# The first batch's softmax over tokens in the other batches' layout, with x loaded ahead of most weights

## The chip, the cores and the metric

The kernel runs on one core of a Trainium2 chip. The metric is the device time of one execution in microseconds, lower is better. The engines are TensorE (PE, with its weight loads PEld), VectorE (DVE), ScalarE (ACT), GpSimd (POOL) and SyncE (SP, which issues the DMAs here).

## The reference

Four sequences of 12608 tokens with 128 channels go through two stages: attention to 32 inducing points, and a channel mix.

```python
B, N, m, C = 4, 12608, 32, 128
scale = 1.0 / np.sqrt(C)
def mab(q, kv):
    s = scale * (q @ kv.transpose(0, 2, 1))
    s = s - s.max(-1, keepdims=True)
    a = np.exp(s)
    a /= a.sum(-1, keepdims=True) + 1e-09
    return a @ kv
h = mab(I, x)            # I: the inducing points; softmax over all tokens
x = mab(x, h)            # softmax over the 32 points, token by token
x_prev = np.concatenate([zeros((B, 1, D)), x[:, :-1, :]], axis=1)
xk = mu_k * x + (1.0 - mu_k) * x_prev
xr = mu_r * x + (1.0 - mu_r) * x_prev
k = np.maximum(xk @ w_k, 0.0)          # w_k: 128 x 1024
v = k * k @ w_v                        # w_v: 1024 x 128
out = 1.0 / (1.0 + np.exp(-(xr @ w_r))) * v
```

x is float32. The weights of the channel mix come as float64; each is turned into float32 on the chip.

## The kernel before

A batch is cut into six blocks of 2048 tokens (four groups of 512) and a tail of 320. Stage A (softmax over tokens) reads a block: x is transposed to channels by tokens (`xt`), the 32 inducing points give scores for four token parts that lie on four sets of 32 partitions, a running maximum is kept, the exponentials are turned back and multiplied with x. Their sum and the product (`acc`) are rescaled when the maximum grows. `combine` makes `hT` and the mixed products `h4k`, `h4r`, from which the folded weights `W` (parts for k, and 128 columns for the gate) are made by `wpart`. Stage B (softmax over the 32 points) gives per group a tile `R`. The channel mix is a loop of 400 units, four for each group: `up` (four matmuls from `R` and `W`), `square` (DVE evacuates with a Relu to `k_t`, ACT squares twice, POOL subtracts to `kl`), and four units later `down`. ScalarE, DVE and POOL all work for each unit, and everything else is hung between units by number (`at`, `soon`).

The order is written out by hand: every engine runs its instructions in the order in which the code issues them. For batches 1 to 3 stages A and B run between the units of the batch before (`stage_a`, `stage_b`). For batch 0 there is nothing to hide behind: `head()` runs its stage A alone, `start()` its first softmax over the points and its weights, and then the units begin. In `head()` the conversion of the float64 weights is also done: `work` is a list of small steps (six for each of five weight parts: exponent L103, mantissa L113, clamp L107, sign L118, low L121, power L125 with POOL's product L131; and two `split_wv` steps), and `place(n)` issues the next n of them. `PARTS` says how many at which point.

In batch 0 the tokens of a group lie 128 apart per step in x's tiles (`(k p) c`, rows of 512 bytes). In batches 1 to 3 a partition holds 16 tokens in a row (`(p s) c`), and the four parts of a block's scores are then not the four groups. Because batch 0's parts had running maxima of their own, `maxes()` takes the maximum over the four parts at the end and `weights()` rescales.

Of the kernel before, what the change touches and what calls it, by code (L numbers as in the profile page):

```python
# [19 lines left out]
def kernel(  # L20
# [62 lines left out]
    def load_weight(dst, src, n, raw):  # L83
# [11 lines left out]
        def steps():  # L95
# [10 lines left out]
            def clamp():  # L106
                v.tensor_scalar(out=X.t, in0=X.t, scalar1=1151.0, scalar2=-896.0, op0=ALU.min, op1=ALU.add)  # L107
                nc.scalar.activation(out=X.t, in_=X.t, func=AF.Relu)
# [101 lines left out]

    def stage_a_head(j):


# [1 line left out]
        first = j == NBLK - 1
        gr = groups(j)
        w = gr[0][1]
        nk = (w + P - 1) // P
        pw = min(w, P)
        L = Batch()  # L220

        def tr():
            for h in range(0, Q, 2):
                ps = pa.tile([P, 2, G], F32, name="ps_a")
                for i in range(2):
                    for k in range(nk):
                        nc.tensor.transpose(out=ps[:, i, k * pw:(k + 1) * pw], in_=S.xn[j, h + i][:pw, k, :],  # L227
                                            identity=ident[:pw, :pw])
                for i in range(2):
                    dst = xt_tile(S, j, h + i)  # L230
                    if h + i > 0 or not first:
                        nc.scalar.copy(out=dst[:, :w], in_=ps[:, i, :w])
# [9 lines left out]
        def maxi():  # L242
            L.mx = sm.tile([P, 1], F32, name="mx1", bufs=4)
            nc.vector.tensor_reduce(out=L.mx, in_=L.s1[:, :w], op=ALU.max, axis=AX.X)
# [3 lines left out]
            nc.vector.tensor_scalar(out=L.nb, in0=L.mx, scalar1=-scale, scalar2=None, op0=ALU.mult)
# [15 lines left out]
        def etrans():  # L264
            L.ep = pb_tile()
            for k in range(nk):
                nc.tensor.transpose(out=L.ep[:pw, k * P:(k + 1) * P],
                                    in_=L.e1t[:, k * pw:(k + 1) * pw], identity=ident)

        def ecopy():  # L270
            L.e1 = st.tile([P, Q, P], F32, name="e1")
            nc.vector.tensor_copy(out=L.e1[:pw, :nk, :],
                                  in_=L.ep[:pw, :nk * P].rearrange("p (k a) -> p k a", a=P))

        def sums():
            if not first:
                nc.vector.scalar_tensor_tensor(out=S.sum, in0=S.sum, scalar=L.al, in1=L.ss,
                                               op0=ALU.mult, op1=ALU.add)

        def hmm():  # L280
            ps = L.hp = pb_tile()
            for k in range(nk):
                for i in range(Q):
                    nc.tensor.matmul(out=ps[M * i:M * (i + 1), :C],
                                     lhsT=L.e1[:pw, k, M * i:M * (i + 1)],
                                     rhs=S.xn[j, i][:pw, k, :],
                                     start=(k == 0), stop=(k == nk - 1))
            for i in range(Q):
                S.xn.pop((j, i), None)

        def acc():
            if first:
                nc.vector.tensor_copy(out=S.acc, in_=L.hp[:, :C])
            else:
                nc.vector.scalar_tensor_tensor(out=S.acc, in0=S.acc, scalar=L.al,
                                               in1=L.hp[:, :C], op0=ALU.mult, op1=ALU.add)
# [2 lines left out]
        L.ecopy, L.sums, L.hmm, L.acc = ecopy, sums, hmm, acc
# [173 lines left out]
    def combine(b, at=None, t=0):  # L473
# [3 lines left out]
        def maxes():  # L477
            bank = next(banks)
            ps = pb_tile(bank)
            nc.tensor.transpose(out=ps[:1, :P], in_=S.mrun, identity=ident)  # L480
            mg = sm.tile([1, M], F32, name="mg")
            nc.vector.tensor_reduce(out=mg, in_=ps[:1, :P].rearrange("p (i m) -> p m i", i=Q), op=ALU.max, axis=AX.X)
            ps2 = pb_tile(bank)
            for i in range(Q):
                nc.tensor.matmul(out=ps2[M * i:M * (i + 1), :1], lhsT=mg, rhs=one, start=True, stop=True)
            nm = sm.tile([P, 1], F32, name="nm")
            nc.vector.tensor_scalar(out=nm, in0=ps2[:, :1], scalar1=-scale, scalar2=None, op0=ALU.mult)
            L["nm"] = nm

        ahead = at is None  # L490

        def weights():
            ws = S.sum
            if ahead:
                wt = sm.tile([P, 1], F32, name="wt")
                nc.scalar.activation(out=wt, in_=S.mrun, func=AF.Exp, bias=L["nm"], scale=scale)
                ws = sm.tile([P, 1], F32, name="ws")
                nc.vector.tensor_tensor(out=ws, in0=S.sum, in1=wt, op=ALU.mult)
            ps = pb_tile(None if ahead else "b")
            nc.tensor.matmul(out=ps[:, :1], lhsT=stack_f, rhs=ws, start=True, stop=True)  # L500
# [570 lines left out]
```

## Time and profile before

| | us |
|---|---|
| median of 3 runs | 1143.24 (1142.75 to 1146.4) |
| span of the profiled execution | 1141.9 |
| PE busy | 1100.8 |
| POOL busy | 948.5 |
| maximum of batch 0's first full block (L244) | 19.78 |
| hT (L521) | 50.13 |
| first evacuation of the loop (L792) | 60.22 |

The profiled execution is one more run: its own time is known as the span, from its first to its last instruction; the three runs of the first row are timed from outside and lie 0.9 to 4.5 us above that span. Rows of a profile name a line of the kernel, the engine, the operation, and the tiles as out<-in; durations are in us, means of one in ns.

### The profile page before, as it was taken

How to read it: one execution, taken by the hardware profiler on the slowest of the kernel's cores; microseconds unless marked ns; L12 is line 12 of the kernel's file. 1: busy time of each engine (PE TensorE's matmuls, PEld its weight loads, DVE VectorE, ACT ScalarE, POOL GpSimd, SP SyncE). 2: the span in 40 equal slices, each digit the busy share in tenths (PEclk: the TensorE clock that was granted, in tenths of full speed). 3: DMA queues.
4: the chain of work that ended last, by engine and by line, in shares of the span. 5: the costliest groups of instructions: out<-in, count | busy, mean ns of one | idle time of the engine just before them, and what ended most of it. 6: DMA issues, size and time to landing. Idle time of an engine off the chain costs nothing.

```text
span 1141.9 us, 17672 instructions
## 1 busy us (share of the span) xinstructions
PE 1100.8 (96%) x5710; PEld 836.7 (73%) x5710; DVE 917.5 (80%) x1294; ACT 971.6 (85%) x1107; POOL 948.5 (83%) x413
## 2 busy tenths in 40 slices
PE   6788999999989999999999999999999999999997
PEld 4466777777777777777777777777778777777886
DVE  4787899887678988887777889898777888887665
ACT  4487888888988888888987988889889988889996
POOL 1157888988877988888889888888888899999996
PEclk9989999999999999999999999999999999999999
DMA  9213454555135455555134455545222233242212
GB/s 268 75 29 92 106 111 108 127 129 106 33 67 119 94 124 123 125 120 124 23 63 86 110 127 121 131 96 125 49 51 60 45 65 59 54 74 56 43 28 34
DMA packets 274988, 102.32 MB, mean 90 GB/s; under 512 B 234288, under 2 KB 249808, under 8 KB 272592
## 3 DMA queue, kind: packets, MB, share of 16 engines
q1 hardware_dynamic: 274560, 101.18, 40.8%
q8 instruction: 45, 0.74, 0.3%
q14 instruction: 47, 0.39, 0.1%
q10 hardware_dynamic: 336, 0.02, 0.0%
HBM read 28.07 MB, written 25.82 MB: 47 GB/s over the span
## 4 chain that ended last, share of the span: by engine, by line
PE 80%; DVE 9%; ACT 7%; issue 3%; DMA 1%; SPq 0%; DVEq 0%; ACTq 0%
PE ps_v L811 40%; PE ps_a L780 15%; PE ps_a L782 13%; DVE k_t L792 3%; PE pb_b L617 2%; PE ps_v L769 2%; PE ps_v L770 2%; PE pb_a L359 2%; PE pb_a L428 2%; ACT kh L797 2%; ACT L772 1%; ACT L634 1%; ACT k_t L798 1%; DVE kh L794 1%; PE ps_a L227 1%
## 5 line engine op out<-in xcount | busy, mean ns | idle before, releaser
L800 POOL TENSOR_TENSOR kl<-k_t,kh 128x1024 fp32r<-128x1024 f32 (+2 forms) x400 | 939.6, 2377 | 151.7 <-ACT k_t L798 131.2
L792 DVE TENSOR_SCALAR k_t<-ps_a 128x1024 f32<-128x1024 f32 (+1 forms) x400 | 480.4, 1201 | 153.9 <-PE ps_a L782 144.2
L798 ACT ACTIVATE k_t<-k_t 128x1024 f32<-128x1024 f32 (+1 forms) x400 | 418.6, 1049 | 38.6 <-DVE kh L794 22.2
L797 ACT ACTIVATE kh<-k_t 128x1024 fp32r<-128x1024 f32 (+1 forms) x352 | 366.1, 1040 | 89.5 <-PE ps_v L811 49.8
L780 PE MATMUL ps_a<-R,W 128*128 128x512 f32 (+1 forms) x800 | 325.2, 407 | 8.8 <-DMA R<-al 4.7
L782 PE MATMUL ps_a<-R,W 128*128 128x512 f32 (+1 forms) x800 | 314.7, 394 | 0.0
L811 PE MATMUL ps_v<-kh,wvh 128*128 128x512 f32 (+1 forms) x800 | 250.2, 394 | 5.3 <-ACT rT L772 4.7
L811 PE MATMUL ps_v<-kl,wvh 128*128 128x512 f32 (+1 forms) x800 | 249.1, 392 | 0.2 <-POOL kl L800 0.2
L811 PE MATMUL ps_v<-kh,wvl 128*128 128x512 f32 (+1 forms) x800 | 249.2, 392 | 0.0
L780 PEld LDWEIGHTS ps_a<-R,W 128*128 128x128 f32 x800 | 151.7, 190 | 82.9 <-issue 20.0
L811 PEld LDWEIGHTS ps_v<-kh,wvh 128*128 128x128 f32 x800 | 149.7, 189 | 44.0 <-ACT rT L772 9.9
L811 PEld LDWEIGHTS ps_v<-kl,wvh 128*128 128x128 f32 x800 | 150.3, 189 | 34.8 <-POOL kl L800 0.4
L811 PEld LDWEIGHTS ps_v<-kh,wvl 128*128 128x128 f32 x800 | 150.6, 189 | 34.2
L782 PEld LDWEIGHTS ps_a<-R,W 128*128 128x128 f32 x800 | 151.7, 190 | 30.8
L816 DVE TENSOR_TENSOR oT<-ps_v,rT 128x512 f32<-128x512 f32 (+1 forms) x100 | 66.7, 667 | 2.3
L827 DVE STREAM_TRANSPOSE ot<-oT 128x512 f32<-128x512 f32 x96 | 67.3, 701 | 0.0
L794 DVE SCALAR_TENSOR_TENSOR kh<-ps_a,k_t 128x1024 fp32r<-128x1024 f32 x48 | 58.8, 1225 | 5.4 <-DVE k_t L792 0.5
L772 ACT ACTIVATE rT<-ps_v 128x512 f32<-128x512 f32 (+1 forms) x99 | 57.3, 579 | 0.3
L331 DVE STREAM_TRANSPOSE xs<-xb 128x512 f32<-128x512 f32 x72 | 50.0, 695 | 3.6 <-DMA xt<-xs 1.8
L769 PE MATMUL ps_v<-R,W 128*128 128x512 f32 (+1 forms) x99 | 39.1, 395 | 1.4 <-DVE oT L816 1.4
L772 ACT ACT_TABLE_LOAD x31 | 39.8, 1283 | 0.5
L770 PE MATMUL ps_v<-R,W 128*128 128x512 f32 (+1 forms) x99 | 38.7, 391 | 0.0
(192 smaller groups left out, 609.5 us busy)
## 6 DMA issues: line engine op xcount, KB each, us to landing
out_dram<-ot SPq DMA_DIRECT2D x184, 128.0 KB, 3.3
xb<-in_x_dram SPq DMA_DIRECT2D x18, 1024.0 KB, 5.5
xt<-xs SPq DMA_DIRECT2D x288, 64.0 KB, 2.0
R<-ah SPq DMA_DIRECT2D x184, 64.0 KB, 2.0
R<-al SPq DMA_DIRECT2D x184, 64.0 KB, 2.0
kh<-in_x_dram SPq DMA_DIRECT2D x4, 512.0 KB, 7.9
kl<-in_x_dram SPq DMA_DIRECT2D x4, 512.0 KB, 7.5
xb<-in_x_dram SPq DMA_DIRECT2D x8, 256.0 KB, 5.3
```

The lines of the kernel that those rows point to most:

```text
L769: nc.tensor.matmul(out=ps[:, :w], lhsT=S.W[0][:, F:WF], rhs=R[:, 1:w + 1], start=True, stop=False)
L772: nc.scalar.activation(out=self.rT, in_=ps[:, :w], func=AF.Sigmoid)
L780: nc.tensor.matmul(out=ps[:, c, :w], lhsT=S.W[0][:, cs], rhs=R[:, 1:w + 1], start=True, stop=False)
L782: nc.tensor.matmul(out=ps[:, c, :w], lhsT=S.W[1][:, cs], rhs=R[:, 0:w], start=False, stop=True)
L792: nc.vector.tensor_scalar(out=k, in0=self.ps[:, :, :w], scalar1=0.0, scalar2=None, op0=ALU.max)
L794: nc.vector.scalar_tensor_tensor(out=kh, in0=self.ps[:, :, :w], scalar=0.0, in1=k, op0=ALU.max, op1=ALU.mult)
L797: nc.scalar.activation(out=kh, in_=k, func=AF.Square)
L798: nc.scalar.activation(out=k, in_=k, func=AF.Square)
L800: return lambda eng, a, z: eng.tensor_tensor(out=kl[:, :, a:z], in0=k[:, :, a:z], in1=kh.bitcast(F32)[:, :, a:z], op=ALU.subtract)
L811: nc.tensor.matmul(out=self.v, lhsT=wt[:, fc, :], rhs=kk[:, c, :], start=(fc == 0 and n == 0), stop=(fc == FC - 1 and n == 2))
L816: nc.vector.tensor_tensor(out=self.oT, in0=self.v, in1=self.rT, op=ALU.mult)
L827: nc.vector.transpose(out=ot[:, o:o + w], in_=self.oT)
```

## The change

Batch 0 gets the layout of the other batches: a block's loads read `(p s) c`, in two halves of eight tokens a partition (block 0 in four quarters), and the loads of x go first, with one weight part behind each of blocks 1 to 3 and the rest last. A block's transposes are copied out by ACT in two instructions of 1024 elements and not four of 512, into one tile for the block. The maximum is joined over the four parts in each block (five one-element steps on DVE), as in the other batches, and `maxes()` and its rescaling go. The turn of the exponentials is done by DVE alone (L282) and not by PE and a copy. The tail has its own small path. The clamp of the weight conversion goes to POOL. In `start()` the first group's softmax runs alone, the second's behind it, with the maxima, sums and quotients in PSUM. The gate's products (`gates`), the conversion of w_r and of the second half of w_v, and both splits move into units 0 and 1 of the loop.

PE at the start of `head()`. kh, kl and xb hold x, xl its tail; ps_a takes transposes, ps_v scores. Before:

```order
L227 MATMUL ps_a<-ident,xl 128x80 x4
L227 MATMUL ps_a<-ident,kh 128x128 x16
L239 MATMUL ps_v<-xtl,indT 32x80 x4
L227 MATMUL ps_a<-ident,kh 128x128 x16
L267 MATMUL pb_b<-ident,rT 80x128
L239 MATMUL ps_v<-xt,indT 32x512 x4
```

And now:

```order
L223 MATMUL ps_a<-ident,xl 128x80 x4
L229 MATMUL ps_a<-ident,kh 128x128 x8
L240 MATMUL ps_v<-xtl,indT 32x80 x4
L229 MATMUL ps_a<-ident,kh 128x128 x8
L240 MATMUL ps_v<-xt,indT 32x512 x4
L277 MATMUL pb_b<-ident,rT 80x128
L229 MATMUL ps_a<-ident,kh 128x128 x16
```

Block 0's scores (32x512) stood behind block 1's transposes; now they stand ahead of them.

DVE in the blocks of `head()`, from one block's turn to the next (s is the tile of the exponents, mkr the joined maximum). Before, one block:

```order
L272 COPY e_317<-pb_b 128x512
L277 SCALAR_TENSOR_TENSOR sum<-sum,alpha,ss 128x1
L244 TENSOR_REDUCE mx_325<-ps_v 128x1
L246 TENSOR_TENSOR mx_325<-mx_325,mx_257 128x1
L248 TENSOR_SCALAR nb<-mx_325 128x1
L103 TENSOR_SCALAR s_335<-k_t 128x512
```

And now:

```order
L282 STREAM_TRANSPOSE e_344<-rT 128x512
L286 TENSOR_SCALAR sum<-sum,alpha,ss 128x1
L246 TENSOR_REDUCE mx_347<-ps_v 128x1
L248 TENSOR_SCALAR mh<-mx_347 64x1
L251 TENSOR_SCALAR mkr<-mh,mkr 32x1
L255 COPY mkr<-mkr 32x1
L256 COPY mkr<-mkr 64x1
L258 TENSOR_SCALAR nb<-mkr 128x1
L125 SCALAR_TENSOR_TENSOR s_299<-s_299,aT 128x512 [waits Activation_49]
L103 TENSOR_SCALAR s_374<-k_t 128x512 [waits DMAHW5_49,Pool_49]
```

The next part's exponent stands behind the last step of the part before and waits for POOL.

POOL from the last conversions of `head()` into the loop (kl is the loop's subtraction, one per unit). Before:

```order
L131 TENSOR_TENSOR ot<-e1t,s_415 128x512 [waits DVE_49]
L131 TENSOR_TENSOR wr_sb<-e1t,s_495 128x128 [waits DVE_49]
L161 TENSOR_TENSOR wvl<-ot,wvh 128x512 [waits Activation_49,Pool_49] x2
L800 TENSOR_TENSOR kl<-k_t,kh 128x1024 [waits DMAHW3_49,PE_49,Activation_49]
L800 TENSOR_TENSOR kl<-k_t,kh 128x1024 [waits DMAHW4_49,PE_49,Activation_49]
```

And now:

```order
L131 TENSOR_TENSOR ot<-e1t,s_472 128x512 [waits DVE_49]
L817 TENSOR_TENSOR kl<-k_t,kh 128x1024 [waits DMAHW3_49,PE_49,Activation_49]
L107 TENSOR_SCALAR s_700<-s_700 128x128 [waits DVE_49,Pool_49]
L131 TENSOR_TENSOR wr_sb<-e1t,s_700 128x128 [waits DVE_49]
L161 TENSOR_TENSOR wvl<-ot,wvh 128x512 [waits Activation_49]
L817 TENSOR_TENSOR kl<-k_t,kh 128x1024 [waits DMAHW4_49,PE_49,Activation_49]
L107 TENSOR_SCALAR s_743<-s_743 128x512 [waits DVE_49]
L131 TENSOR_TENSOR ot<-e1t,s_743 128x512 [waits DVE_49]
L161 TENSOR_TENSOR wvl<-ot,wvh 128x512 [waits Activation_49]
L817 TENSOR_TENSOR kl<-k_t,kh 128x1024 [waits DMAHW6_49,PE_49,Activation_49]
```

Two conversions and both splits now stand among the first three kl, their clamps (L107) each behind one. On DVE the steps of w_r (s_700) and the gate products (h4r) stand between the first two evacuations:

```order
L809 TENSOR_SCALAR k_t<-ps_a 128x1024
L540 TENSOR_TENSOR W_630<-ps_v,W_630 64x512
L732 TENSOR_REDUCE pb_b<-s_637 128x4
L733 TENSOR_SCALAR sm_692<-pb_b 128x4
L734 RECIPROCAL pb_b<-sm_692 128x4
L735 TENSOR_TENSOR pb_b<-s_637,pb_b 128x128
L540 TENSOR_TENSOR W_631<-ps_v,W_631 64x512
L103 TENSOR_SCALAR s_700<-oT 128x128
L113 TENSOR_SCALAR xs<-oT 128x128
L118 TENSOR_SCALAR aT<-oT 128x128
L121 SCALAR_TENSOR_TENSOR e1t<-oT,e1t 128x128
L125 SCALAR_TENSOR_TENSOR s_700<-s_700,aT 128x128
```

Before, one W low part alone stood there (L544 between two L792); the gate products, the next L809 and then the same five steps of w_v (s_743) follow.

The core of the diff:

```diff
-    xt_pool = ctx.enter_context(tc.tile_pool(name="xt_pool", bufs=24))
+    xt_pool = ctx.enter_context(tc.tile_pool(name="xt_pool", bufs=6))
...
             def clamp():
-                v.tensor_scalar(out=X.t, in0=X.t, scalar1=1151.0, scalar2=-896.0, op0=ALU.min, op1=ALU.add)
+                nc.gpsimd.tensor_scalar(out=X.t, in0=X.t, scalar1=1151.0, scalar2=-896.0, op0=ALU.min, op1=ALU.add)
                 nc.scalar.activation(out=X.t, in_=X.t, func=AF.Relu)
...
+        src = x[b, j * BLK:(j + 1) * BLK, :].rearrange("(p s) c -> p s c", p=P)
...
+        n = 2 * Q // pieces
+        for h in range(2):
+            for o in range(0, 2 * Q, n):
+                nc.sync.dma_start(out=S.xh[j][h][:, o:o + n, :], in_=src[:, 2 * Q * h + o:2 * Q * h + o + n, :])
...
-                for i in range(2):
-                    dst = xt_tile(S, j, h + i)
-                    if h + i > 0 or not first:
-                        nc.scalar.copy(out=dst[:, :w], in_=ps[:, i, :w])
...
+            nc.scalar.copy(out=S.xtb[j][:, :, h * G // 2:(h + 1) * G // 2].rearrange("c i (s q) -> c i s q", q=M),
+                           in_=ps.rearrange("c a n -> c (a n)").rearrange("c (s i q) -> c i s q", i=Q, q=M))
...
+            v.tensor_reduce(out=mx, in_=L.s1[:, :w], op=ALU.max, axis=AX.X)
+            mh = sm.tile([half, 1], F32, name="mh", bufs=1)
+            v.tensor_scalar(out=mh, in0=mx[:half], scalar1=mx[half:], scalar2=None, op0=ALU.max)
...
+            v.tensor_copy(out=L.mx[M:half], in_=L.mx[:M])
+            v.tensor_copy(out=L.mx[half:], in_=L.mx[:half])
...
-            L.ep = pb_tile()
-            for k in range(nk):
-                nc.tensor.transpose(out=L.ep[:pw, k * P:(k + 1) * P],
-                                    in_=L.e1t[:, k * pw:(k + 1) * pw], identity=ident)
...
+            L.e1 = st.tile([P, Q, P], F32, name=("e1", "al")[k % 2]).rearrange("p k (i m) -> p (k i) m", m=M)
+            v.transpose(out=L.e1, in_=L.e1t.rearrange("p (s q) -> p s q", q=M))
...
-    for k, j in enumerate(order_h):
-        load_x(0, j, pairs if j < 4 else None)
-        if wloads:
+    load_x(0, NBLK - 1)
+    for j in range(NBLK - 1):
+        load_x(0, j, pairs if j < 4 else None, 2 if j == 0 else 1)
+        if 1 <= j <= 3:
             wloads.pop(0)()
     run(wloads)
...
-    for f in conv.values():
-        work += f
-    work += [lambda c=c: split_wv(c) for c in range(FC // cg)]
+    for f in (("k", 0), ("k", 1), ("v", 0), ("r", 0), ("v", 1)):
+        work += conv[f]
+    work.insert(24, lambda: split_wv(0))
+    work.append(lambda: split_wv(1))
...
+        for k in range(last):
+            bl[k + 1].tr(0)
             if k > 0:
...
+                bl[k - 1].etrans()
+                bl[k - 1].sums()
+            bl[k].maxi()
+            bl[k + 1].tr(1)
+            bl[k].expo()
+            place((0, 3, 2, 3, 2)[k])
...
+            bl[k + 1].scores()
+            (bl[k - 1] if k > 0 else tl).acc()
+            place((0, 2, 2, 2, 2)[k])
...
+        run([sc0, tu0, df0, ex0, sc1, wa[0][0], wa[1][0], tu1, nm0, wa[0][1], hi0, wa[1][1], lo0, wa[0][2], put0,
+             df1, ex1, wa[1][2]])
+        for f in (wb[0][0], wb[0][1], wb[1][0], wb[1][1]):
             soon(0, f)
...
+        for n, f in ((0, wb[0][2]), (0, nm1), (0, hi1), (0, wb[1][2]), (0, lambda: place(7)), (0, gates),
+                     (1, lo1), (1, sc2), (1, lambda: place(7)), (2, tu2), (2, df2), (2, ex2),
+                     (3, nm2)):
             at(n, f)
```

More of the change, by code (lines that the diff above doesn't have):

```diff
@@ L211, in stage_a_head @@
-    def stage_a_head(j):
-        S = batches[0]
[L215 to L219, printed above, removed]
-        L = Batch()
-        def tr():
-            for h in range(0, Q, 2):
-                ps = pa.tile([P, 2, G], F32, name="ps_a")
-                for i in range(2):
-                    for k in range(nk):
-                        nc.tensor.transpose(out=ps[:, i, k * pw:(k + 1) * pw], in_=S.xn[j, h + i][:pw, k, :],
-                                            identity=ident[:pw, :pw])
-                for i in range(2):
-                    dst = xt_tile(S, j, h + i)
-                    if h + i > 0 or not first:
-                        nc.scalar.copy(out=dst[:, :w], in_=ps[:, i, :w])
-                    else:
-                        nc.vector.tensor_copy(out=dst[:, :w], in_=ps[:, i, :w])
+        if pair is not None:
+            S.xh[j] = [next(pair).rearrange("p u (k c) -> p (u k) c", c=C) for _ in range(2)]
+        else:
+            t = xn_pool.tile([P, Q * Q, C], F32, name="xb")
+            S.xh[j] = [t[:, :2 * Q, :], t[:, 2 * Q:, :]]
@@ L280, in hmm @@
-        def hmm():
-            ps = L.hp = pb_tile()
-            for k in range(nk):
-                for i in range(Q):
[L284 to L289, printed above, removed]
+            if tail:
+                ps = pb_tile("b")
+                nc.tensor.transpose(out=ps[:w, :P], in_=L.e1t[:, :w], identity=ident)
+                L.e1 = sm.tile([P, P], F32, name="mk", bufs=1)
+                v.tensor_copy(out=L.e1[:w], in_=ps[:w, :P])
+                return
@@ L298, in stage_a_head @@
+            if not tail:
+                S.xh.pop(j)
         L.tr, L.scores, L.maxi, L.expo, L.etrans = tr, scores, maxi, expo, etrans
[L299 removed]
+        L.sums, L.hmm, L.acc = sums, hmm, acc
         return L
@@ L475, in combine @@
         L = {}
[L477 to L488, printed above, removed]
         ahead = at is None
         def weights():
[L493 to L500, printed above, removed]
+            ps = pb_tile("a" if ahead else "b")
+            nc.tensor.matmul(out=ps[:, :1], lhsT=stack_f, rhs=S.sum, start=True, stop=True)
             rd = sm.tile([P, 1], F32, name="rd")
@@ L744, in put @@
                                         in_=X["a"].bitcast(F32)[:, c].rearrange("p q m -> p (q m)"))
-                nc.scalar.copy(out=S.R[g][:, 1:G + 1], in_=ps)
+                nc.scalar.copy(out=S.R[g][:, 1:G + 1].rearrange("r (p s) -> r p s", p=M),
+                               in_=ps.rearrange("r (s p) -> r p s", p=M))
             return high, low, put
-        return scores, diff, expo, norm, [place(k) for k in range(len(gs))]
+        return part, [place(k) for k in range(len(gs))]
     NG = (NBLK - 1) * Q + 1
```

264 lines of the change are left out of this document (149 added, 115 removed).

## The prediction

> **What bounds the kernel now.** I read the page first, then the busy time by stretches, then the chain of waits through the first 86 us, then instructions in order of time and the groups by shape.
>
> ```profile
> span 1141.9 us, 17672 instructions
> PE 1100.8 (96%) x5710; PEld 836.7 (73%) x5710; DVE 917.5 (80%) x1294; ACT 971.6 (85%) x1107; POOL 948.5 (83%) x413
> ```
>
> ```profile
> 20.00:30.00 10.00, 8.41 (x104) 5.72 (x107) 9.86 (x24) 7.86 (x18) 2.30 (x2) 1.00 1.12 298
> ...
> 58.00:74.00 16.00, 12.87 (x58) 9.49 (x58) 14.58 (x21) 12.03 (x19) 7.89 (x4) 0.79 0.04 8
> 74.00:100.00 26.00, 24.92 (x118) 18.17 (x116) 23.02 (x29) 23.15 (x26) 19.03 (x9) 1.00 0.27 77
> 100.00:400.00 300.00, 293.17 (x1519) 221.57 (x1515) 249.86 (x354) 258.51 (x289) 256.04 (x109) 0.99 0.46 100
> ```
>
> The columns are the stretch, PE, PEld, DVE, ACT, POOL, granted clock, DMA share and GB/s. From 100 us on PE is busy 293 of 300 us, so a unit of the main loop costs what PE needs, and time lost before it is not won back there. The edits all lie in the first 75 us, where DVE holds the chain: 9.86 of 10 us from 20 to 30, 14.58 of 16 from 58 to 74. So the question is how much later or earlier the loop reaches its pace. I mark this by DVE's evacuations (L792 before, L809 after: one per unit, first instruction behind PE's up products).
>
> ```profile
> 1.67 7.79 DMA kh<-in_x_dram
> ...
> 19.78 0.70 DVE mx L244
> ...
> 43.42 0.61 DVE mx L244
> ...
> 50.13 0.29 DVE hT L521
> ...
> 50.94 0.52 DVE h4r L515 x2
> ...
> 59.03 0.43 DVE al L737
> ...
> 59.49 0.70 DVE W L544
> ...
> 60.22 1.23 DVE k_t L792
> ...
> 64.27 2.09 DVE s L711
> ```
>
> ```profile
> 66.28 1.21 DVE L792 TENSOR_SCALAR k_t<-ps_a 128x1024 f32<-128x1024 f32 x1
> ...
> 85.39 1.21 DVE L792 TENSOR_SCALAR k_t<-ps_a 128x1024 f32<-128x1024 f32 x1
> ```
>
> Milestones before: first full block's maximum 19.78, sixth block's 43.4, hT 50.13, first evacuation 60.22, third 66.28, ninth 85.39.
>
> **The change, part by part.** Six terms, each between two milestones.
>
> *To the first block's maximum.* PE, in order of time:
>
> ```profile
> 9.60 3.65 PE L227 MATMUL ps_a<-ident,kh 128*128 128x128 f32 x16 [5.43 <-DMA kh<-in_x_dram]
> ...
> 14.38 3.73 PE L227 MATMUL ps_a<-ident,kh 128*128 128x128 f32 x16 [0.71 <-ACT xt L232]
> ...
> 18.25 1.45 PE L239 MATMUL ps_v<-xt,indT 128*32 128x512 f32 x8
> ...
> 25.36 2.08 PE L227 MATMUL ps_a<-ident,kl 128*128 128x128 f32 x16
> ```
>
> The second row is block 1, and it stands ahead of block 0's scores (18.25). After the change block 0's scores come right behind its own transposes, and block 0 takes the place of the first w_k half in the queue. The first kh landed at 9.46 (1.67 + 7.79) with the tail, half of w_k and itself to move, 1.21 MB; tail and block 0 are the same 1.21 MB, in rows of 2 KB and not 512 B. I take 8.8 for its last quarter (bounds 7.5 and 9.46). Then four transposes at 3.65/16 us, one joined copy of about 1.0 (estimate, from the 1024-element ACT rows below), so scores at about 11. They run at the slow rate the first two rows show (0.23 us a transpose, against 0.13 in the last), 2.1 us and not 1.45, and the tail's small copy stands ahead of the maximum on DVE: 14.0, against 19.78. **-5.8.** The other loads move behind x (w_k behind blocks 1 and 2, the first w_v half behind block 3, the rest last); the first conversion starts in block 1's period, past 20 us, when its weights have long landed at the 298 GB/s shown. SP issues four loads for blocks 4 and 5 and not eight, and waits there for earlier landings alone; batch 1's first load still waits for the products on block 4's buffer. A joined token tile comes free only when all four groups of its block are scored, block 0's in unit 1, and batch 1 first writes one in unit 3: no wait.
>
> *First to sixth maximum.* Groups of DVE up to 58 us (mean ns of one behind the comma):
>
> ```profile
> L244 DVE TENSOR_REDUCE mx<-ps_v 128x1 f32<-128x512 f32 x6 | 4.1, 683 | 1.3 <-PE ps_v L239 1.3
> L277 DVE SCALAR_TENSOR_TENSOR sum<-sum,alpha,ss 128x1 f32<-128x1 f32 x6 | 3.6, 596 | 0.0
> L272 DVE COPY e<-pb_b 128x512 f32<-128x512 f32 x5 | 3.4, 687 | 1.6 <-PE pb_b L267 1.5
> L121 DVE SCALAR_TENSOR_TENSOR e1t<-k_t,e1t 128x512 f32<-128x512 uint32 x4 | 2.8, 693 | 5.9 <-ACT e1t L114 5.9
> L125 DVE SCALAR_TENSOR_TENSOR s<-s,aT 128x512 int32<-128x512 int32 x4 | 2.7, 685 | 0.0
> L295 DVE SCALAR_TENSOR_TENSOR acc<-acc,alpha,pb_a 128x128 f32<-128x128 f32 x6 | 2.0, 342 | 0.3 <-PE pb_a L284 0.3
> L103 DVE TENSOR_SCALAR s<-k_t 128x512 int32<-128x512 int32 x4 | 1.7, 428 | 3.4 <-DMA k_t<-in_moe_w_k_dram 3.4
> ...
> L248 DVE TENSOR_SCALAR nb<-mx 128x1 f32<-128x1 f32 x7 | 1.1, 154 | 0.2
> ...
> L125 DVE SCALAR_TENSOR_TENSOR s<-s,aT 128x128 int32<-128x128 int32 x1 | 0.3, 284 | 0.0
> ```
>
> ```profile
> L331 DVE STREAM_TRANSPOSE xs<-xb 128x512 f32<-128x512 f32 x7 | 4.9, 699 | 0.5 <-DMA R<-al 0.4
> ```
>
> Per block DVE had copy 0.69, sum 0.60, maximum 0.68, two one-element steps of 0.15, acc 0.34: 2.6. It gets a turn of 0.70 (L331's shape), a one-element sum 0.15, maximum 0.68, five one-element steps that each wait for the one before, 0.20 apart, and acc 0.34: 2.87. Five periods: +1.3. Weight conversion: three of six instructions (four of L103's kind, 0.43, and 0.69 + 0.69: 3.1) and the small one of w_r (128 columns, L125 0.28, six of about 0.25: 1.5) become three of five (2.67), the clamp being on POOL: -2.8. A new wait: in two blocks the next exponent (L103) stands straight behind L125, writes the tile that POOL's product is still reading, and so holds DVE for POOL's 1.28 us, with the next block's turn and maximum queued behind it: +2.6. And the first of the five periods is no longer DVE's: block 1's transposes at the slow rate (3.7), two joined copies, scores: 5.4 where DVE needs 2.87: +2.5. **+3.6**: 27.2 and not 23.6. The joined copies save ACT little (two of about 1.0 for four of half that), and nothing on this path.
>
> *Sixth maximum to hT.* Maximum and five small steps 1.7, exponentials 0.96, turn 0.70, the block's products 1.08, acc 0.34, last product 0.5, hand-overs 0.1: 5.4, against 6.7 before, since the reduction of the maximum over the four parts (L480 to L498) is gone. **-1.4.**
>
> *hT to the first evacuation.* Before 10.1. The two h4r products (0.52) go behind it; al's low part (0.43) and one W low part (0.70) now follow it; half-width softmax steps take about 0.29 and not 0.42, seven of them on the path, -0.9; the other half's turn and maximum stand between, +0.3 net of the exponential they cover. Sum -2.25, with R's copy issued earlier **-2.4**: 7.7.
>
> So the first evacuation comes at 54.2 and not 60.2, 6.0 earlier.
>
> *First to third evacuation.* Here the moved conversions of w_r and half of w_v stand (one after each of units 0 and 1), their clamp now on POOL.
>
> ```profile
> L800 POOL TENSOR_TENSOR kl<-k_t,kh 128x1024 fp32r<-128x1024 f32 x4 | 9.7, 2427 | 22.7 <-ACT k_t L798 21.5 <-PE ps_a L782 1.2
> L131 POOL TENSOR_TENSOR ot<-e1t,s 128x512 f32<-128x512 f32 x2 | 2.6, 1278 | 7.9 <-DVE s L125 7.9
> ...
> L131 POOL TENSOR_TENSOR wr_sb<-e1t,s 128x128 f32<-128x128 f32 x1 | 0.5, 459 | 2.9 <-DVE s L125 2.9
> masks.py:199 POOL TENSOR_SCALAR_AFFINE_SELECT ident<-ident 128x128 f32<-128x128 f32 x1 | 0.3, 294 | 0.1
> ```
>
> ```profile
> L798 ACT ACTIVATE k_t<-k_t 128x1024 f32<-128x1024 f32 x5 | 5.3, 1060 | 0.2
> L797 ACT ACTIVATE kh<-k_t 128x1024 fp32r<-128x1024 f32 x5 | 5.3, 1056 | 1.8 <-DVE k_t L792 1.7
> ...
> L541 ACT CAST W<-ps_v 128x512 fp32r<-128x512 f32 x2 | 1.2, 589 | 1.4 <-PE ps_v L538 1.4
> ```
>
> ```profile
> L108 ACT ACTIVATE s<-s 128x512 int32<-128x512 int32 x4 | 2.5, 623 | 0.0
> ...
> L108 ACT ACTIVATE s<-s 128x128 int32<-128x128 int32 x1 | 0.3, 297 | 0.0
> ```
>
> POOL's queue has kl of unit 0, then w_r's clamp; kl of unit 1, then w_v's clamp. DVE's has L125 of each conversion ahead of the next evacuation, L125 needs ACT's Relu, and the Relu needs the clamp. So evacuation n+1 waits for kl of unit n, which in turn starts only after evacuation n and both squares. A ring, with nothing beside it. First lap: evacuation 1.23, two W casts ahead on ACT 1.1, squares 1.06 + 1.06, kl 2.43, clamp 0.3, Relu 0.3, L125 0.28, the two gate products 0.45: 8.2. Second: 1.23 + 1.06 + 1.06 + 2.43 + clamp + 0.62 + 0.68 = 7.1 + clamp. No row shows a clamp of 512 on POOL. Two inputs cost 0.459 at 128 and 1.278 at 512, so 0.19 fixed; one input at 128 took 0.294, so 0.8 ns an element more: 0.6 at 512. The ends are 0.3 (the 128 row) and 1.28 (two inputs at 512); I take 0.6, the row with one input. Lap 7.7. Together 15.9, against 6.1: **+9.9**. PE has little to do then and waits with it: the products for unit 2 stand behind a score that needs DVE's step after the second evacuation. The 2.09 us of L711 (its two inputs in SBUF, while POOL ran kl) goes, since the softmax keeps one operand in PSUM; this is inside the 6.1.
>
> *Third to ninth.* POOL still owes w_v's product and split, 2 x 1.28, ahead of kl of unit 2; before 19.1, now about 19.7. **+0.6.**
>
> Sum: -5.8 + 3.6 - 1.4 - 2.4 + 9.9 + 0.6 = **+4.5 us** on a profiled execution with a span of 1141.9. The runs' median, 1143.24, lies 1.3 above that span, with nothing in the change that would alter the part around it: 1143.24 + 4.5 = **1147.7**.
>
> [...] The first two PE rows run at half the rate of the last: PE was at work from 9.6, with a break of 0.7 at 13.7, and was still at half rate 8 us later. [...]
>
> **Rivals.**
>
> *Early clock.* PE is warm before block 1: for it, work starts at 6 and not at 9.6; against, pieces arriving 0.9 us apart leave breaks, as in the first 9 us before. Saving 16 x (0.23 - 0.13) = 1.6 in the transposes and 1.3 in scores and the rest, 2.9: +1.6, 1144.8, no change that shows. [...] An earlier landing (7.5) gives 1.3 alone and also points there. With it goes the mild case that the ring costs a little less than I reckon.
>
> *The loop catches up.* This ends faster. If the shortfall of the first units is regained behind unit 2, only the 6.0 us of the head is left: 1137.2. For it: from the third evacuation to the ninth a unit takes 19.1/6 = 3.2 us, while kl needs 2.43. Regaining 10.5 us at 0.75 a unit takes 14 units. Against it: PE is busy 24.92 of 26 us from 74 to 100 and 293 of 300 after, so there is no slack to draw on. It decides for faster if over 8 of the 10.5 come back.
>
> *A dear clamp.* POOL handles integers at the cost of a kl, 2.4. The second lap grows by 1.8, and the three conversions in the blocks wait for their clamps too, 0.8 each: +8.7, 1151.9. No row has an integer on POOL.
>
> **How the numbers follow.** 0.3% (3.4 us) is about what a measurement of this kernel can tell from no change. Forecast, between 3.4 and 7 us slower (1146.7 to 1150.2): 0.50. Dear clamp or more: 0.13. Early clock and the like, within 3.4: 0.24. Catching up, faster: 0.13. Slower 0.63, same 0.24, faster 0.13. The range leaves out the faster case and the far end of the dear one: 1140.0 to 1151.5.
>
> **What would show it.** In the new profile: block 0's maximum near 14 and block 5's near 41; hT near 46.5; evacuations (L809) near 54, 62.5 and 70, ninth near 90; each of the first two kl on POOL followed by a clamp and only then DVE's L125; PE idle some 7 us between the products of units 1 and 2, and its clock low after that. I am wrong if L809's third start lies before 66, if hT is before 43, or if the ninth evacuation lies nearer to 85 although the third is late.

## The result and the profile after

The changed kernel took 1152.50 us (median of 4 runs, 1148.26 to 1153.99), the one before 1142.99: ratio 1.0077, interval 1.0052 to 1.0102. In a second comparison it was 1153.89 against 1143.81, ratio 1.0110 (1.0093 to 1.0128). Forecast were 1147.7 and a range up to 1151.5: the direction is right, the size is not. The span and busy time of the profiled execution, which took 1148.26 and was the quickest of the four:

```profile
span 1146.3 us, 17583 instructions
PE 1095.8 (96%) x5675; PEld 831.6 (73%) x5675; DVE 920.2 (80%) x1315; ACT 970.4 (85%) x1092; POOL 957.1 (83%) x418
```

This span is 4.4 above the one before, close to the prediction's sum of 4.5, and the agreement is an accident. The milestones, DVE in order of time (start, duration):

```profile
13.05 0.68 DVE L246 TENSOR_REDUCE mx<-ps_v 128x1 f32<-128x512 f32 x1
...
39.69 0.68 DVE L246 TENSOR_REDUCE mx<-ps_v 128x1 f32<-128x512 f32 x1
...
46.24 0.29 DVE L516 COPY hT<-pb_a 128x128 f32<-128x128 f32 x1 [0.89 <-PE pb_a L514]
...
55.24 1.23 DVE L809 TENSOR_SCALAR k_t<-ps_a 128x1024 f32<-128x1024 f32 x1 [1.05 <-PE ps_a L799]
...
73.43 1.22 DVE L809 TENSOR_SCALAR k_t<-ps_a 128x1024 f32<-128x1024 f32 x1
...
93.64 1.21 DVE L809 TENSOR_SCALAR k_t<-ps_a 128x1024 f32<-128x1024 f32 x1
```

The same milestones in the kernel before and in a second profile of the change (the run `again` below), and what each stretch lost or gained against before:

| stretch, ending at | before | after | second profile | forecast | measured, two profiles |
|---|---|---|---|---|---|
| block 0's maximum | 19.78 | 13.05 | 13.82 | -5.8 | -6.7, -6.0 |
| block 5's maximum | 43.35 | 39.69 | 42.06 | +3.6 | +3.1, +4.7 |
| hT | 50.13 | 46.24 | 48.31 | -1.4 | -0.2, -0.5 |
| first evacuation | 60.22 | 55.24 | 57.44 | -2.4 | -1.1, -1.0 |
| third evacuation | 66.28 | 73.43 | 75.61 | +9.9 | +12.1, +12.1 |
| ninth evacuation | 85.39 | 93.64 | 95.80 | +0.6 | +1.1, +1.1 |
| sum so far | | | | +4.5 | +8.2, +10.4 |
| last evacuation | 1131.10 | 1135.75 | 1141.36 | 0 | -3.6, -0.1 |

So the first 94 us lost 8 to 10 us, as the timed runs say, and the first profile won 3.6 of them back in the loop, which the second did not. The busy time by stretches has the place (stretch, its length, PE, PEld, DVE, ACT, POOL, granted clock, DMA share, GB/s):

```profile
30.00:40.00 10.00, 6.83 (x73) 3.85 (x77) 8.01 (x23) 6.03 (x12) 4.23 (x3) 0.83 0.00 1
40.00:51.00 11.00, 7.24 (x93) 4.18 (x85) 6.55 (x25) 1.27 (x4) 0.34 (x1) 0.72 0.26 97
58.00:74.00 16.00, 5.00 (x32) 3.57 (x32) 10.69 (x18) 6.11 (x10) 9.67 (x7) 0.79 0.00 1
74.00:100.00 26.00, 22.50 (x96) 16.76 (x97) 21.42 (x34) 21.68 (x28) 18.96 (x9) 0.93 0.29 81
```

From 58 to 74 PE works 5.0 of 16 us (12.87 before). The chain of waits there is the ring of the prediction, step for step. Its second lap (start, duration, what):

```profile
64.04 1.14 DVE k_t L809
65.20 1.07 ACT kh L814
66.29 1.07 ACT k_t L815
67.43 2.37 POOL kl L817
69.88 2.26 POOL s L107
72.16 0.64 ACT s L108
72.82 0.70 DVE s L125
```

Only the clamp (L107) is not what was forecast. POOL's groups by shape up to 76 us, mean ns of one behind the comma:

```profile
L107 POOL TENSOR_SCALAR s<-s 128x512 int32<-128x512 int32 x4 | 8.2, 2055 | 19.4 <-DVE s L103 19.3
...
L131 POOL TENSOR_TENSOR wk_sb<-e1t,s 128x512 f32<-128x512 f32 x2 | 2.5, 1273 | 6.5 <-DVE s L125 6.5
...
L107 POOL TENSOR_SCALAR s<-s 128x128 int32<-128x128 int32 x1 | 0.6, 640 | 0.1
```

2.05 us at 512 columns, 0.64 at 128, where 0.6 and 0.3 were taken.

### The profile page after: what moved, and what is told of

It is laid out like the page before. It is cut to its first block, busy times and chain, and to the rows that moved or that the text cites. A ratio compares the mean times of both kernels' runs of the same rounds, so it can differ in the third digit from the quotient of the medians.

```text
span 1146.3 us, 17583 instructions
## 1 busy us (share of the span) xinstructions
PE 1095.8 (96%) x5675; PEld 831.6 (73%) x5675; DVE 920.2 (80%) x1315; ACT 970.4 (85%) x1092; POOL 957.1 (83%) x418
## 4 chain that ended last, share of the span: by engine, by line
PE 77%; ACT 9%; DVE 7%; issue 3%; POOL 2%; DMA 1%; SPq 1%; DVEq 0%; ACTq 0%; POOLq 0%
PE ps_v L828 39%; PE ps_a L797 14%; PE ps_a L799 13%; DVE k_t L809 3%; ACT kh L814 2%; PE pb_a L374 2%; PE pb_b L613 2%; PE ps_v L786 2%; PE ps_v L787 2%; PE pb_a L443 2%; ACT L789 1%; ACT k_t L815 1%; ACT L630 1%; POOL kl L817 1%; DVE kh L811 1%
## 5 line engine op out<-in xcount | busy, mean ns | idle before, releaser
L809 DVE TENSOR_SCALAR k_t<-ps_a 128x1024 f32<-128x1024 f32 (+1 forms) x400 | 480.2, 1201 | 153.4 <-PE ps_a L799 137.7
L828 PE MATMUL ps_v<-kl,wvh 128*128 128x512 f32 (+1 forms) x800 | 246.2, 389 | 1.2 <-POOL kl L817 1.2
```

The lines of the kernel that those rows point to most:

```text
L809: nc.vector.tensor_scalar(out=k, in0=self.ps[:, :, :w], scalar1=0.0, scalar2=None, op0=ALU.max)
L828: nc.tensor.matmul(out=self.v, lhsT=wt[:, fc, :], rhs=kk[:, c, :], start=(fc == 0 and n == 0), stop=(fc == FC - 1 and n == 2))
```

## The experiments

Times stand beside the kernel before in the same comparison. Kernels of one comparison can be set against each other by their times; across comparisons, only their ratios to the kernel before can. Milestones are of one profile each (columns as above, "laps" is first to third evacuation).

| kernel | median us | before | hT | first evacuation | laps | ninth |
|---|---|---|---|---|---|---|
| again | 1153.89 | 1143.81 | 48.31 | 57.44 | 18.2 | 95.80 |
| clamp_dve | 1149.14 | 1143.81 | 45.85 | 54.86 | 14.7 | 89.69 |
| conv_head | 1147.10 | 1143.81 | 50.73 | 59.74 | 8.9 | 88.07 |
| conv_head_dve | 1143.98 | 1143.81 | 47.36 | 56.66 | 9.2 | 86.25 |
| warm | 1152.34 | 1142.45 | 46.76 | 57.48 | 18.2 | 95.86 |
| late_scores | 1153.15 | 1142.45 | 46.45 | 55.45 | 18.2 | 93.83 |
| both_late | 1141.89 | 1142.45 | 47.93 | 58.10 | 6.8 | 84.96 |
| both_gaps | 1139.82 | 1142.45 | 46.82 | 56.02 | 6.0 | 82.06 |
| warm2 | 1151.13 | 1142.58 | 48.24 | 56.76 | 19.2 | 96.15 |
| gaps_warm | 1140.29 | 1142.58 | 47.08 | 56.00 | 6.8 | 82.88 |
| gaps_warm_sc | 1138.57 | 1142.58 | 46.20 | 54.70 | 6.8 | 81.57 |
| before_pool | 1147.53 | 1142.58 | 52.82 | 64.29 | 6.1 | 89.48 |

**again**: no edit.

> The changed kernel as it is, once more. In its first profile the ninth evacuation came at 93.64 us against 85.39 before (8.25 later), but the span ended only 4.4 later; the timed runs say 9.5. Theory LOOP: the loss of the first units is 8.2 in every execution, and the loop behind them varies by chance, so this profile has its third evacuation at 73 to 74 and its ninth at 93 to 94.2 whatever its total is, and a total 3 to 5 us above the first one's shows behind 100 us. Theory START: executions differ in the first 100 us (clock, landings), the loop takes the same 1042 us from ninth to last evacuation as in the first profile, and a longer total goes with a ninth evacuation 3 to 5 us later. Median expected by both: 1150 to 1153.

Each theory holds in part, neither alone. Against LOOP's 93 to 94.2 the ninth evacuation is at 95.80, 2.2 later, so the start varies; from ninth to last the loop took 1045.6, not 1042.1 (1045.7 before), so it varies too. The stretches ahead of and in a dip of the clock (columns as above), of the second profile and of the one before:

```profile
345.82:349.23 3.41, 1.20 (x6) 1.05 (x7) 0.88 (x2) 2.26 (x4) 3.41 (x4) 1.00 0.41 98
349.23:352.64 3.41, 3.41 (x12) 2.95 (x11) 2.00 (x3) 1.99 (x2) 1.45 (x1) 0.50 0.37 82
```

```profile
104.42:107.83 3.41, 1.02 (x5) 0.52 (x5) 2.60 (x6) 2.90 (x3) 3.41 (x2) 1.00 0.34 80
107.83:111.24 3.41, 3.41 (x9) 2.65 (x10) 1.44 (x2) 0.00 (x0) 3.41 (x2) 0.50 0.35 77
336.53:339.94 3.41, 1.07 (x5) 0.61 (x4) 1.68 (x4) 3.06 (x6) 3.41 (x3) 1.00 0.42 100
339.94:343.35 3.41, 3.41 (x12) 2.95 (x11) 1.84 (x2) 0.79 (x1) 2.26 (x2) 0.50 0.29 63
```

Near 345 such a dip made six units 1.5 us longer (18.9 to 19.0 us, against 17.4 in the first profile of the change, which has none there). The profile before has two, each profile of the change one. That is 1.5 of the 3.6 (the second profile lost as much elsewhere); the rest lies in small differences between units 140 and 272 and stays open.

**clamp_dve**: one edit of the change undone.

```
-                nc.gpsimd.tensor_scalar(out=X.t, in0=X.t, scalar1=1151.0, ...)
+                v.tensor_scalar(out=X.t, in0=X.t, scalar1=1151.0, ...)
```

> The changed kernel with one edit undone: the clamp of the weight conversion is on DVE again, not on POOL. Theory RING with the dear clamp: in the profile of the change the clamps took 2.03, 1.92, 2.02 and 2.25 us on POOL, and from the first to the third evacuation the time was 18.2 us against 6.1, because the clamp stands behind kl. Without it on POOL the wait for kl of the unit before goes: third evacuation near 68 and not 73.4, ninth near 88 and not 93.6, and the time 5 to 7 us under the change's, about 1146. Theory HEAD (the clamp is covered, the loss is the conversions' DVE work and the waits of the head): the third evacuation moves by less than 1.5, and the time stays within 2 us of the change's.

4.75 us under `again`; laps 14.7, third evacuation 69.52. HEAD (within 2) falls. In the head the clamp cost only 0.4: block 5's maximum is at 39.31, against 39.69 in the first profile of the change, which like this one has a single dip of the clock there (the second has one of twice the length). But 8.6 of the 12.1 us stay without a clamp on POOL, and the rows of DVE and of POOL say why:

```profile
59.70 2.13 DVE L121 SCALAR_TENSOR_TENSOR e1t<-oT,e1t 128x128 f32<-128x128 uint32 x1 [0.22 <-ACT e1t L114]
...
64.73 0.42 DVE L107 TENSOR_SCALAR s<-s 128x512 int32<-128x512 int32 x1
...
66.54 2.44 DVE L121 SCALAR_TENSOR_TENSOR e1t<-k_t,e1t 128x512 f32<-128x512 uint32 x1 [1.06 <-ACT e1t L114]
```

```profile
59.28 2.41 POOL L817 TENSOR_TENSOR kl<-k_t,kh 128x1024 fp32r<-128x1024 f32 x1 [19.33 <-ACT k_t L815]
...
66.07 2.37 POOL L817 TENSOR_TENSOR kl<-k_t,kh 128x1024 fp32r<-128x1024 f32 x1 [2.27 <-ACT k_t L815]
```

L121 has two inputs in SBUF and takes 0.29 (128 columns) and 0.69 (512) in the profile before, where POOL rests; beside kl (59.28 to 61.69, 66.07 to 68.44) it ends only behind kl. So the next evacuation waits for kl even without the clamp.

**conv_head**: the conversions of units 0 and 1 back in the head.

```
-            place((0, 3, 2, 3, 2)[k])      ...   place((0, 2, 2, 2, 2)[k])
+            place((0, 3, 3, 3, 3)[k])      ...   place((0, 3, 3, 3, 4)[k])
+        place(3)   # behind bl[last].expo()
+        place(4)   # behind bl[last].sums()
-        (0, lambda: place(7)), ... (1, lambda: place(7)),
```

> The changed kernel with the conversions of w_r and of the second half of w_v, their splits with them, in the head's blocks again (one half conversion in each half of a block) and none in units 0 and 1; the clamp stays on POOL. Theory RING: first to third evacuation falls from 18.2 to 7 to 9 us; the head grows by the DVE work of 4.2 us and waits for dear clamps, so the first evacuation comes at 58.5 to 60.5 and not 55.2; third near 68; net 4 to 6 us under the change. Theory HEAD: the head's growth eats it all, since POOL's 2 us clamp stands in every conversion there: third evacuation at 72 or later, time within 2 us of the change's.

6.8 under `again`, laps 8.9, first evacuation 59.74: RING, a little over its gain.

**conv_head_dve**: both edits.

> Both edits together: conversions in the head, clamp on DVE. Theory RING: no conversion waits for POOL's kl, no L125 for a clamp on POOL: first evacuation at 55 to 57, third near 63, ninth near 84; 9 to 11 us under the change, 1142 to 1144, level with the kernel before or a little under. If the two edits take away the same wait, the sum is not that of the two kernels' gains: then 6 to 7 and not 10. Theory HEAD: DVE holds the head, five clamps of 0.43 and one of 0.23 more make it longer than with POOL: first evacuation after 60, time no better than that of either edit alone.

9.9 under `again` and level with before (ratio 1.0004, 0.9992 to 1.0017). The single gains, 4.75 and 6.8, add up to 11.5, so by the medians they share 1.6 (3.3 by the ratios). The third evacuation came at 65.89, not 63, because PE stood still ahead of the scores of groups 2 and 3, and worked at half rate behind (clock 0.50 from 62.3 to 69.1):

```profile
62.77 1.08 PE L704 MATMUL pb_b<-xt,hT 128*32 128x128 f32 x16 [3.50 <-DVE al L753]
```

They write the bank from which DVE's low part (L753) of group 1 still reads.

**warm**: transposes that nothing reads, to keep PE busy.

```
+                fill(L.hp[:, C:2 * C], n)      # hmm:    n = 10 (k == 3), 13 (block 4)
+            fill(L.s1[:, :P], n)               # scores: n = 14 (k == 3)
-        spin(6)
+        spin(18)
+  8 transposes into L["ps"] ahead of the second group's scores
```

> The changed kernel with extra transposes of the identity on PE, whose results nothing reads: 10 and 14 ahead of the products and scores of the fourth of the blocks' periods, 13 ahead of the products on block 4, 18 for 6 ahead of the last ones, 8 ahead of the second group's scores. They stand where PE waited 1.3 to 1.8 us in the change's profile, whose granted clock was 0.50 from 32 to 35 and from 46 to 51. Theory CLOCK: these waits are what lowers the clock, and the half rate lies on the path (scores 1.94 for 1.06, the W products 3.29 for some 1.9): with the fill the clock is 1.00 up to 58, the first evacuation comes at 53 to 54 and not at 55.2 or 57.4, and the time is 1.5 to 3 us under the change's. Rival WAITS: PE is not on the path there, DVE and ACT are; first evacuation at 55 or later, since the fill delays what it stands ahead of, and no gain in time. First to third evacuation stays at 18 by both.

The dip at 31 is gone (clock 1.00 from 20 to 48), and hT comes between those of the two profiles of the change (46.24 and 48.31), but the first evacuation at 57.48: the eight last transposes waited for DVE themselves and pushed the scores back, and the clock fell at 48.4. The run decides nothing on the path from hT.

**late_scores**: `(1, sc2)` becomes `(2, sc2)` in the changed kernel.

> The changed kernel with the scores of groups 2 and 3 issued in unit 2, behind its up products, and not in unit 1. In the change's profile they waited 7.7 us on PE for DVE's low part of group 1, which reads the bank that they write, and the up products of unit 2 stood behind them. Theory RING: the third evacuation waits for POOL's clamp and DVE's L125 (72.8) and not for PE (up products done at 68.4), so nothing is gained: third evacuation 18 us behind the first, time within 1.5 us of the change's. Rival PE ORDER: this wait is the loss; the third evacuation comes 3 us or more earlier and the time falls by as much.

Nothing gained: third evacuation 18.2 behind the first. PE's wait was beside the ring, as RING has it.

**both_late**: the same edit in conv_head_dve.

> The same move of the scores in the kernel with the conversions in the head and the clamp on DVE. There the ring is gone, and PE idles 3.5 us ahead of those scores, with the third evacuation waiting for PE from 62.7 to 65.9. Theory: here the move pays what it could not pay beside the ring: first to third evacuation 6 to 7 and not 9.2, clock of 58 to 74 near 1.00 and not 0.79, time 2.5 to 4.5 us under conv_head_dve, 1139.5 to 1141.5. Rival: the next wait (the scores' bank, still read by the second group's low part, now ahead of unit 3) takes it back behind the third evacuation: ninth evacuation 20 us behind the third, and no gain in time.

Laps 6.8 and not 9.2, and the ninth evacuation 1.3 earlier. The time is 2.1 us lower by the medians, but these are of two comparisons: the ratios to the kernel before, 1.0004 (0.9992 to 1.0017) and 0.9991 (0.9973 to 1.0009), are 1.5 us apart and their intervals overlap. So the laps show the edit worth nothing beside the ring and 2.4 us without it; the 2.5 us or more of time that were expected are not shown.

**both_gaps**: both_late with the last steps of a conversion moved into DVE's waits behind hT.

```
-        place(4)                               # ahead of hT
+  run([... wa[1][1], lambda: place(2), lo0, ... wa[1][2], lambda: place(1)])
+  (0, lambda: place(1))                        # unit 0, the split
-                X.t = st.tile([P, G], I32, name="s2")[:, :n]
+                X.t = st.tile([P, G], I32, name="xs", bufs=3)[:, :n]
```

> both_late with the last four steps of the second w_v half's conversion (sign, low part, power, split) taken from ahead of hT into DVE's waits behind it, and the exponents in a tile of their own. In conv_head_dve these steps and a stack product of 1.12 us instead of 0.28, beside POOL's product, stood between the last maximum and hT (7.9 us against 6.55 in the change). Expected: last maximum to hT back to 6.5, hT to first evacuation 9.0 to 9.6, first evacuation 1 to 1.5 earlier than both_late's, and the time with it, about 1139. Rival: POOL's product and split now stand ahead of kl of unit 0 and DVE's steps ahead of W's low part: first evacuation no earlier, and the second later by 1 or more.

Last maximum to hT 6.3 as expected, first evacuation 2.1 earlier than both_late's (1 to 1.5 expected), laps 6.0, 1139.82; 0.9969 of before (0.9953 to 0.9985).

**warm2, gaps_warm, gaps_warm_sc**: the fill with the eight in a bank of their own, where they wait for nothing, in the changed kernel (warm2) and in both_gaps (gaps_warm); gaps_warm_sc has the second group's scores in their place.

```
+        spin(3)
         hfin()
+        spin(2)
-        run([sc0, tu0, df0, ex0, sc1, ...
+        run([sc0, lambda: spin(8), tu0, df0, ex0, sc1, ...     # warm2, gaps_warm
+        run([sc0, sc1, tu0, df0, ex0, ...                      # gaps_warm_sc
```

> The changed kernel with the fill of the run warm, but none that waits for DVE: instead 3, 2 and 8 transposes of the identity in a bank of their own behind the last products of stage A, behind hT and behind the first group's scores. In the traces so far the granted clock falls to 0.50 for 3.41 us or a multiple of it, right behind a stretch of 3.41 us in which PE was busy less than about 2.2 us. Theory CLOCK: with PE busy over 2.5 us of every 3.41 from 20 to 58 the clock stays 1.00 there, hT to first evacuation falls from 9.0 to 6.8 to 7.5 (four W products at full rate, 1.9 for 3.3 to 3.8, and scores and transposes), first evacuation at 52.5 to 54.5, the time 1.5 to 3 us under the change's. Rival: the path from hT to the first evacuation is DVE's and ACT's, and 9.0 stays 8.5 or more at full clock. The ring's 18 us stay by both.

> both_gaps with such a fill (11 transposes ahead of the products in the fourth and fifth period, 17 ahead of those on block 4, 18 for 6, then 3, 2 and 8 as in warm2). In both_gaps the clock was 0.50 from 40.3 to 43.7 and from 47.1 to 54.0. Theory CLOCK: first evacuation 1.5 to 2.5 earlier than both_gaps's 56.0, third near 60, time 1 to 2.5 us under both_gaps: 1137.5 to 1139. Rival: as much is lost to the fill itself, time within 1 us of both_gaps's.

> gaps_warm with the second group's scores straight behind the first's, ahead of DVE's turn, in place of the 8 transposes. Those scores waited 1.1 us for the first group's difference, which reads the bank that they write, and the W products stood behind them. Expected: the W products start 1 us earlier, the first group's softmax 0.3 later at its turn and 0.4 to 0.7 earlier at its end; first evacuation 0.3 to 0.8 earlier than gaps_warm's, time the same or 0.5 less. Rival: the turn of the first group now waits for both groups' scores, and the W products were covered by DVE anyway: first evacuation no earlier.

The clock of warm2, then of gaps_warm_sc:

```profile
20.00:55.23 35.23, 30.58 (x383) 21.33 (x380) 26.67 (x82) 18.10 (x35) 9.79 (x6) 1.00 0.27 95
51.82:55.23 3.41, 1.78 (x8) 0.71 (x6) 2.66 (x7) 2.11 (x5) 0.00 (x0) 1.00 0.00 0
55.23:58.64 3.41, 3.41 (x7) 2.00 (x7) 1.22 (x1) 0.18 (x1) 0.00 (x0) 0.50 0.02 5
```

```profile
20.00:52.80 32.80, 27.62 (x367) 19.87 (x365) 28.73 (x93) 19.23 (x40) 5.54 (x5) 1.00 0.29 103
49.39:52.80 3.41, 0.78 (x5) 0.58 (x5) 3.26 (x8) 1.65 (x4) 0.00 (x0) 1.00 0.00 0
52.80:56.22 3.42, 3.42 (x7) 1.91 (x8) 2.08 (x3) 0.00 (x1) 1.28 (x1) 0.50 0.00 0
58.00:74.00 16.00, 11.20 (x66) 7.08 (x65) 13.78 (x28) 14.53 (x21) 12.95 (x6) 1.00 0.15 35
```

The fill holds the clock at 1.00 to 55.2 and 52.8. Yet hT to first evacuation stays 8.5 in warm2 (9.0 to 9.1 without), where CLOCK said 6.8 to 7.5, and gaps_warm gains nothing over both_gaps. That does not clear the clock: the dip came later but still ahead of the first evacuation (56.76 and 54.70), and it now holds the up products, which end the path. Two of them in the kernel before, at full rate, and in gaps_warm_sc:

```profile
58.60 0.40 PE L782 MATMUL ps_a<-R,W 128*128 128x512 f32 x1
58.84 0.40 PE L780 MATMUL ps_a<-R,W 128*128 128x512 f32 x1
```

```profile
53.61 0.63 PE L803 MATMUL ps_a<-R,W 128*128 128x512 f32 x1
54.03 0.63 PE L805 MATMUL ps_a<-R,W 128*128 128x512 f32 x1
```

In warm2 the two groups' scores took 0.43 each and not 0.65, and the cast of the first group's quotient (`ah`) followed at once and not 0.7 later, behind the cast of W: 1.1 won. From the first up product to the evacuation it took 1.99 and not 1.44: 0.5 lost again. So by these rows half rate costs that path of the change about 1.1 us, an estimate; no run had the whole path at full rate, and whether the rest is DVE's and ACT's, as the rivals had it, stays open. The scores moved forward brought the first evacuation 1.3 earlier and, with 1138.57, the lowest median: 0.9954 of before (0.9936 to 0.9971), an interval that overlaps those of gaps_warm and both_gaps.

**before_pool**: the kernel before, with only the clamp on POOL.

> The kernel before with one edit of the change alone: the clamp on POOL. There all conversions stand in the head's blocks, with no kl on POOL. Theory RING: the clamp's 2 us are dear only behind kl; here POOL is idle, the four steps of 0.43 and one of 0.23 leave DVE, and L125 waits for the clamp about 1 us in some conversions: first evacuation between 58.5 and 61.5, time within 1.5 us of before. Theory DEAR ANYWHERE: each of five conversions holds DVE by the 2 us less what stands between: first evacuation at 63 or later, and the time 3 us or more over before.

Here my RING theory missed, and DEAR ANYWHERE held: 5.0 us more by the medians (3.4 by the ratio, 1.0030, 1.0011 to 1.0048), first evacuation 64.29. The clamp is dear without any kl, because DVE's L125 waits for it in the blocks:

```profile
L107 POOL TENSOR_SCALAR s<-s 128x512 int32<-128x512 int32 x3 | 6.1, 2024 | 6.9 <-DVE s L103 6.9
```

```profile
23.80 0.69 DVE L125 SCALAR_TENSOR_TENSOR s<-s,aT 128x512 int32<-128x512 int32 x1 [0.92 <-ACT s L108]
```

First to sixth maximum grew by 2.9; the other 1.4 lies between hT and the first evacuation, where the clock was 0.50 from 53.6 to 60.4.

## Why the prediction was right and wrong, point by point

*To block 0's maximum*: right, and better in the first profile, since PE reached full rate in time for block 0's scores (1.07 us). In the second it did not (1.93), 0.8 later. The rival of the early clock thus fits the first profile (block 1's transposes took 1.91, where 3.7 was taken) and the second in part (2.58). What it won, here and in block 1's period below, is 2.0 and 0.7 of its 2.9 us, and no part of the loss.

*First to sixth maximum*: right in size (3.1 and 4.7 for 3.6), in part by luck: the first of the five periods took 4.3 and 4.9 us where 5.4 was taken, the other four 22.4 and 23.3 where 21.8 were. Of the two waits of L103 for POOL's product, forecast at 1.28 each, the profile shows 1.39 and 1.13. Not forecast: the clock falls to half rate at 31 us, because the lighter blocks leave PE idle (busy 1.08 of the 3.41 us ahead, first row below; with the fill of warm the clock is 1.00 there). A single dip cost little there: the stretch took 26.6 us in the first profile and 26.7 in warm without it, but 28.2 in the second profile, whose dip lasted 6.83.

```profile
27.76:31.17 3.41, 1.08 (x32) 0.81 (x32) 3.23 (x11) 3.02 (x5) 0.98 (x1) 1.00 0.02 5
31.17:34.58 3.41, 3.31 (x15) 1.64 (x16) 2.28 (x7) 1.54 (x5) 2.24 (x2) 0.50 0.01 2
```

*Sixth maximum to hT* failed by 1.2: "hand-overs 0.1". The products are two halves of 0.64 with the product of the weights, 0.38, between them, the last one runs at half rate in the first profile (0.80 and not 0.5), and the hand-overs come to 0.3 or more. That hT came at 46.24 where 46.5 was forecast is luck: 0.9 and 0.5 won before made up for the 1.2.

*hT to first evacuation* failed by 1.3: "the other half's turn and maximum stand between, +0.3 net". The second group's scores wait for the first group's difference, and the W products, at half rate, stand behind them. The half rate (clock 0.50 from 44.8 to 51.7), at which the prediction had nothing, is about 1.1 of it by the estimate under warm2; the scores moved forward took 0.4 (8.5 in gaps_warm_sc, 8.9 in gaps_warm). The rows:

```profile
48.40 0.65 PE L704 MATMUL pb_b<-xt,hT 128*32 128x128 f32 x8 [1.16 <-DVE s L720]
48.98 3.29 PE L534 MATMUL ps_v<-wk_sb,h4k 128*128 128x512 f32 x4
```

*First to third evacuation* is the step that failed most: 12.1 for 9.9 (its own laps, 15.9 less 6.1, give 9.8). The mechanism is right to the instruction, the term that failed is the clamp, taken as 0.6 "the row with one input" between 0.3 and 1.28. It took 2.25 there and 0.64 at 128: laps of 8.7 and 9.5 for 8.2 and 7.7, 2.0 of the 2.3 us missed. All its bounds came from rows in float; none held an integer. The rival that priced it at 2.4 gave 1151.9, within 0.6 of the result, in part by luck: of the 2.4 us that this rival adds in the blocks clamp_dve shows 0.4, and the misses at hT and at the first evacuation stand in their place. It deserved more than 0.13, since no row spoke against it. clamp_dve and before_pool show the edit worth 4.75 and 4.95 us in time by the medians (6.4 and 3.4 by the ratios), about half of the whole loss, and conv_head_dve shows the place of the conversions worth the other half. A second gap: the prediction counted the 2.09 us of L711 as gone, which holds for the softmax (L735, with one operand in PSUM, took 0.43 at 128x256 beside kl, at 79.3 in the change), and the same hold came back twice at L121: 2.06 and 2.44 us in the change, under the clamp's wait, and 2.13 and 2.44 in clamp_dve, on the path.

*Third to ninth*: near, +1.1 where +0.6 was forecast.

*The sum against one span*: adding 4.5 to a median took the loop as fixed. It varies by execution: 1042.1 to 1049.0 from ninth to last evacuation over the fourteen profiles. The measured medians fit the sum at the ninth evacuation (8.2 to 10.4), not the one span.

*The loop catches up* fell: the loss at the ninth evacuation stood at 8.2 still at the sixteenth (104.06 before, 112.29 after).

## What to carry to other kernels

Before work is moved to another engine, find a row of that engine with the same type and width; where there is none, the bound is open upwards, and a rival with the dear price deserves more than a small chance. A producer and a consumer that wait for each other through three engines cost their whole lap (here 8.7 and 9.5 us), and a better order elsewhere (late_scores) shows nothing until that ring is cut. Compare milestones, not spans: one span of 1150 hid 3.6 us of the loss here behind a quicker loop, while the ninth evacuation told it.

## What the runs showed of the hardware

In the profiles of the kernel before and of the change, every dip of the granted clock to 0.50 that ended before the span did lasted 3.41 us or 6.83, and in each of the two the dips began whole multiples of 3.41 us apart: at 66.87, 107.83 and 339.94 before, at 31.17, 44.82, 61.89, 75.54 and 116.50 in the change. In `again` (from 62.5) and conv_head_dve (from 45.2) one lasted 10.2, three times 3.41.

Cut into such stretches of 3.41 us, in step with its dips, a profile shows what PE worked in each. Between 20 and 1130 us of the two profiles, every stretch at full clock with up to 1.34 us of PE work was followed by half rate. So were stretches with 1.66 (the change, from 41.41), 1.78 (warm2, from 51.82) and 2.21 (both_gaps, from 43.71), while 1.48 (warm, from 58.60), 1.65 and 1.83 (the change, from 38.00 and 68.72) and 1.94 (before, from 53.22) were not. Half rate ended after stretches with 2.90 us of work (the change, from 75.54) and 2.7 (conv_head_dve, from 52.04), and went on after 2.61 (before, from 66.87) and 3.09 (warm, from 48.36). These stretches give no single amount of work that decides. In 3.41 us of half rate six units of the loop lost 1.5 us near 345.

An integer clamp with one input cost POOL 2.05 us at 512 columns in the change, 1.6 times its product of two float inputs (1.27) and 4.9 times DVE's 0.42 for the same instruction in clamp_dve. Whether the integers cost it or the two steps (a minimum and an addition) that the instruction takes, no run separates.
